# Softmax attention with a convolution beside it: conversion buffers in three spans, a longer late ring, 480 conversions

## The chip, the cores and the metric

The kernel runs on one core of one Trainium2 chip, in one launch. The core has five engines that run their own instruction queues and meet only at semaphores: TensorE (PE) for matmuls, VectorE (DVE), ScalarE (ACT), GpSimd (POOL) and SyncE (SP), which here only starts transfers. Matmuls write to PSUM; DVE and ACT read it, POOL does not use it in this kernel. The metric is the device time of one execution in microseconds (us), the median of several.

## The reference

```python
g = sigmoid((x * gate_w).sum(-1))                       # one gate a row
qkv = x @ wqkv                                          # x: 2048 x 512, 32 heads of 16
a = softmax(q @ k.T * 16 ** -0.5) @ v  ->  a @ wo       # each head 2048 x 2048
K = einsum("dn,dnl,dn->dl", C, exp(dt * A * l), dt * B).real   # 512 channels, 2048 long, 128 modes
b = causal_convolution(x, K) + x * Dskip
out = g * a + (1 - g) * b
```

The heavy part is the softmax: 32 x 2048 x 2048 exponentials. The second branch builds a convolution kernel K for each of the 512 channels out of powers of complex numbers, and applies it.

## The kernel before

**Attention.** Scores are computed in tiles of 128 keys x 512 queries of one head. A quad is four tiles: four heads on the same keys, one in each strip of 32 rows of PE. There are 512 quads (`NQ`), so 2048 tiles, in 32 blocks of 16 quads (a block is four heads and one quarter of the queries). The tiles stand in a list, three to a group; there are 683 groups (`NG`). `qk` computes the three score tiles of a group into one of two PSUM buffers (SC0 for even groups, SC1 for odd ones). `ex` (line 1037) turns them into bf16 exponentials with one ACT instruction, into slots of a ring. The ring is ET with `NS` slots of 512 columns, and from group `NSG` on also EX, which extends it to `NS2` slots. `seat` hands out the slots; a group's slots must lie together and may not straddle the border of ET and EX. `pv` multiplies the four tiles of a quad with the values (VE) and adds to the accumulator OA. The main loop at the end of `record` makes sure, before `ex` of a group, that the quads whose slots it overwrites have been through `pv`.

**Conversions.** Some tiles do not go to ACT. In a group that takes part, only two tiles are given to ACT, and the third is converted on DVE: `bits` (line 1059) computes scale x score + offset from PSUM into 16-bit integers, whose bits read as bf16 are already a rough exponential. Four converted tiles, the four heads of one quad, fill one buffer DZ; that is a set, and it takes part in four consecutive groups. `batch` (line 1078) makes three copies DU of the whole set with constants added to the integers, on POOL (in the last few groups on DVE, line 1074), and `sums` multiplies all four, DZ and the three DU, with the values, so that the errors of the four average out. Each set thus costs four conversions, three POOL adds and four quads of matmuls, and saves ACT four tiles.

**When a set may start.** `decide` builds the list of tiles as the main loop goes. `win` says in which span of groups (`WIN`: from, to, number of DZ buffers, number of DU buffers) a group lies, whether four groups have passed since the last set, whether the number of sets is below the pace (`PACE`, interpolated over groups), and whether the buffer is free (`room`). `DVCAP` bounds how much idle time of DVE may be used up, `STRX`, `STRE` and `STRK` say where a set may start near the end of a block.

**The convolution.** It is background work, laid between the groups: `params`, `bases`, `tables` and `kstage` build K in four quarters of four blocks of 32 channels (DVE products, among them the T products of line 1132, then matmuls into the PSUM buffer MB, then writes to DRAM); `xrows`, `yloads` and `ystage` load rows of x and of K (buffers U and H) and do the convolution in 32 units of 128 matmuls (`MB<-U,H`). At the end `outs` multiplies with `wo` and adds both branches. DMA starts of all of this go through SP's queue.

**What sets the order.** The kernel is a planner. Every piece of background work is a Python generator that announces an engine and a cost. `Sched.fill` simulates the five engines with fixed durations and, after each group's exponential, issues whatever fits until the time of the next; `Sched.force` issues work early when something is needed. Priorities are the numbers given at the start of each thread. So the order of every engine's queue is fixed when the kernel is built, and constants such as `TP`, `KP`, `OUTP`, `YLP`, `XGO`, `BG1` or `KEEP` only move work within it. PE also gets matmuls on a zero tile (`zero`, tile `wm`), so many that a target (`FILL`, after group `ZEND` `LOW`) of PE activity per group is met; `REST` forces a target on some groups up to a given one.

Of the kernel before, what the change touches and what calls it, by code (L numbers as in the profile page):

```python
# [15 lines left out]
S = 2048  # L16
# [40 lines left out]
NS = 20  # L57
NS2 = 24
NSG = 395
# [14 lines left out]
BG1 = 'g20'  # L74
BG2 = 'K3'
BG3 = 'K3'
TP = 0.86
KP = 0.85
NB = 2
NT = 2  # L80
TB = 4
# [3 lines left out]
US = [2, 12, 3]  # L85
HS = [4, 44, 8]
BACK = 0.66
# [12 lines left out]
KEEP = 8  # L100
FORE = 12
# [3 lines left out]
DVCAP = 8.7  # L105
# [5 lines left out]
STRX = 460  # L111
STRE = 640
# [642 lines left out]
def record(nc, p, B, ins):  # L755
# [7 lines left out]
    NSL = 4 * NQ  # L763
# [132 lines left out]
    plan = dict(q=0, at=0, used=0.0, prev=None, wait={}, x=0)  # L896
# [12 lines left out]
    def win(x):  # L909
        return next((w for w, (lo, hi, *_) in enumerate(WIN) if lo <= x < hi and x >= plan["x"] + 4 and len(sets) < due(x) and room(w)), None)  # L910

    def decide(g):
        while len(tiles) < min(3 * g + 3, NSL):
# [3 lines left out]
            if q + 2 < NQ and (kt < DVK - 1 or STRX <= x < STRE and kt in STRK) and win(x) is not None and idle() >= plan["used"] \  # L917
                    and (kt < DVL or not sets or f"dvp{len(sets) - 1}" in sch.flag):
                w = win(x)
                plan["x"] = x  # L920
                c = next(y for y in range(q, q + 3) if 0 < y % 16 < 15)
                a, b = [y for y in range(q, q + 3) if y != c]
# [3 lines left out]
                for _ in range(12):  # L926
                    if len(tiles) % 3 == 2:
                        vec[len(tiles) // 3] = (len(sets), k)
                        k += 1
                        tiles.append(late.pop(0))  # L930
                    else:
                        tiles.append(own.pop(0))
                plan["wait"][c // 16] = f"dvp{len(sets)}"
                n = sum(st["w"] == w for st in sets)
                r, nu = f"{w}{n % WIN[w][2]}", WIN[w][3]
# [15 lines left out]
            while todo and 4 * todo[0][0] + 3 in home:  # L951
                sch.add(pvq(*todo.pop(0)), 0, True)
# [1097 lines left out]
```

## Time and profile before

| | |
|---|---|
| median of 3 executions | 744.12 us (743.63, 744.12, 1048.6) |
| the profiled execution | 744.34 us |
| its span, first to last instruction | 742.5 us |
| granted TensorE clock, mean | 0.996 of full speed |
| conversions (line 1059) | 464, mean 684 ns |
| POOL adds (line 1078) | 345, mean 1045 ns |
| DMA | 94.89 MB, 128 GB/s over the span |

One of the three executions took 1048.6 us; the other two agree within 0.1%, and the median is one of them. The rows of the profile read as follows: a group of instructions has its line, engine, operation, `out<-in` by the names of the program, the tile shapes and the count; then the busy time of the group in us and the mean length of one instruction in ns; then the idle time of the engine just before them and what ended it. "PEld" is the loading of weights. Where instructions of one engine overlap, the busy time of a group is less than its count times the mean. A row of stretches gives from:to in us, the length, and busy times (with counts) of the engines that appear, then the granted clock, the share of DMA time and GB/s. A row of waits gives who waited for whom, us in total, times, and the longest.

### The profile page before, as it was taken

Reading aid. Unit: us, or ns where it says so; the run is one execution under the profiler, and the core shown is the slowest. Engines: PE = TensorE matmul, PEld = TensorE weight load, DVE = VectorE, ACT = ScalarE, POOL = GpSimd, SP = SyncE. Lnnn points to the kernel's source line nnn. Section 1 sums busy time; section 2 is a strip of 40 time slices with the busy share of each in tenths; the row PEclk is TensorE's granted clock in tenths of the full one; section 3 lists DMA queues with packets and bytes.
Section 4 is the critical chain, followed back from the end, with each engine's and each line's share of the span. In section 5 each row is a group of like instructions: output and inputs, shape, how many; then the busy total and the mean of one; then the engine's idle time right before and its main releaser. Section 6 shows DMA issues by size and latency. Waiting matters only on the chain.

```text
span 742.5 us, 31758 instructions
## 1 busy us (share of the span) xinstructions
PE 688.9 (93%) x14153; PEld 297.9 (40%) x14154; DVE 659.5 (89%) x1109; ACT 728.8 (98%) x696; POOL 363.1 (49%) x365
## 2 busy tenths in 40 slices
PE   8888788888899989999999999999999999999997
PEld 4333333333444444445444544544444442222222
DVE  6999999999999999899998988877888888898886
ACT  7999999999999999999999999999999999999996
POOL 4000000000026436555557556677888888888783
PEclk9999999999999999999999999999999999999999
DMA  9647931224656673343788586458877661001001
GB/s 217 154 108 164 177 40 41 62 52 130 167 128 183 175 214 84 91 126 80 214 226 228 156 221 170 130 112 198 218 159 183 164 153 49 19 19 27 19 15 38
DMA packets 148702, 94.89 MB, mean 128 GB/s; under 512 B 88338, under 2 KB 130004, under 8 KB 148564
## 3 DMA queue, kind: packets, MB, share of 16 engines
q1 hardware_dynamic: 147604, 91.99, 50.2%
q8 instruction: 111, 1.82, 1.1%
q10 hardware_dynamic: 960, 0.85, 0.4%
q14 instruction: 27, 0.22, 0.1%
HBM read 63.94 MB, written 18.90 MB: 112 GB/s over the span
## 4 chain that ended last, share of the span: by engine, by line
ACT 89%; PE 9%; DVE 1%; POOL 1%; issue 0%; DVEq 0%
ACT ET L1037 84%; ACT EX L1037 5%; PE SC L770 4%; PE OA L770 3%; PE MB L770 2%; POOL DU L1078 1%; DVE DZ L1059 0%; DVE Qm L1908 0%; DVE VE L880 0%; DVE Ks L1510 0%; DVE fo L2009 0%; DVE B L1341 0%; DVEq L732 0%; DVE wm L824 0%; DVE KT L1911 0%
## 5 line engine op out<-in xcount | busy, mean ns | idle before, releaser
L1037 ACT ACTIVATE ET<-SC 128x1024 bf16<-128x1024 f32 (+1 forms) x637 | 685.0, 1321 | 2.2 <-PE SC L770 1.9
L1078 POOL INT64_ADD DU<-DZ x345 | 355.6, 1045 | 364.5 <-DVE DZ L1059 263.8
L1059 DVE TENSOR_SCALAR DZ<-SC 128x512 uint16<-128x512 f32 x464 | 310.5, 684 | 60.0 <-PE SC L770 55.9
L770 PE MATMUL SC<-Qm,KT 32*128 32x512 bf16 x2048 | 271.6, 385 | 11.0 <-ACT ET L1037 7.5
L770 PE MATMUL OA<-ET,VE 128*32 128x512 bf16 x1490 | 153.5, 388 | 30.1 <-ACT ET L1037 29.4
L770 PEld LDWEIGHTS SC<-Qm,KT 32*128 32x128 bf16 x2048 | 68.9, 91 | 194.4 <-ACT ET L1037 124.6
L770 PE MATMUL OA<-DU,VE 128*32 128x512 bf16 x1392 | 134.5, 387 | 1.1 <-POOL DU L1078 1.1
L770 PEld LDWEIGHTS MB<-U,H 128*32 128x32 bf16 x4096 | 91.1, 143 | 29.3 <-issue 13.4
L770 PE MATMUL MB<-U,H 128*32 128x128 bf16 (+7 forms) x4096 | 96.5, 223 | 0.0
L770 PEld LDWEIGHTS OA<-ET,VE 128*32 128x32 bf16 x1490 | 39.6, 95 | 95.5 <-ACT ET L1037 52.0
L770 PE MATMUL OA<-wm 128*32 128x256 bf16 (+3 forms) x527 | 74.5, 344 | 1.2 <-DVE idf L825 1.2
L1132 DVE TENSOR_TENSOR T<-B,DT 128x1536 bf16<-128x1536 bf16 x64 | 62.3, 1013 | 0.0
L770 PEld LDWEIGHTS OA<-DU,VE 128*32 128x32 bf16 x1392 | 35.4, 95 | 50.9 <-issue 43.3
L1037 ACT ACTIVATE EX<-SC 128x1024 bf16<-128x1024 f32 (+1 forms) x46 | 50.5, 1227 | 0.0
L770 PEld LDWEIGHTS MB<-T,Z 128*32 128x32 bf16 x2048 | 42.1, 156 | 11.7 <-issue 9.0
L770 PE MATMUL MB<-T,Z 128*32 128x64 bf16 (+1 forms) x2048 | 45.9, 236 | 0.3 <-issue 0.3
L770 PE MATMUL OA<-DZ,VE 128*32 128x512 bf16 x464 | 45.8, 384 | 0.0
L1132 DVE TENSOR_TENSOR ft<-Z 128x512 f32<-128x512 f32 (+3 forms) x48 | 38.7, 829 | 0.3
L1132 DVE TENSOR_TENSOR Z<-ft,ft 128x1024 bf16<-128x1024 bf16 (+3 forms) x56 | 33.3, 595 | 0.5
L1099 DVE STREAM_TRANSPOSE OT<-OA 128x512 f32<-128x512 f32 x32 | 22.7, 709 | 1.8 <-PE OA L770 1.8
L770 PEld LDWEIGHTS OA<-wm 128*32 128x32 bf16 (+2 forms) x527 | 20.4, 96 | 9.4 <-issue 6.4
L1613 DVE TENSOR_TENSOR Yst<-MB,gt 128x512 bf16<-128x512 f32 x32 | 21.8, 680 | 1.8 <-PE MB L770 1.7
(141 smaller groups left out, 407.6 us busy)
## 6 DMA issues: line engine op xcount, KB each, us to landing
H<-gm_kd SPq DMA_DIRECT2D x128, 256.0 KB, 3.9
U<-gm_xs SPq DMA_DIRECT2D x128, 134.2 KB, 3.9
T<-B SPq DMA_DIRECT2D x16, 256.0 KB, 3.1
gm_yd<-Yst SPq DMA_DIRECT2D x16, 256.0 KB, 4.2
gm_kd<-Ks SPq DMA_DIRECT2D x64, 40.0 KB, 2.4
gm_xs<-xP SPq DMA_DIRECT2D x16, 136.0 KB, 7.0
gm_pd<-L SPq DMA_DIRECT2D x8, 256.0 KB, 3.6
Z<-gm_pd SPq DMA_DIRECT2D x8, 256.0 KB, 3.7
```

The costliest lines, as they stand in the source:

```text
L770: op("PE", lambda t: t.matmul(out(), lhsT(), rhs(), start=start, stop=stop, skip_group_check=True, **kw), R, W, c=c, lat=.15, a=a, cfg=cfg)
L1037: op("ACT", lambda a: a.activation(E(at, [[1, 512 * n]]), sc(0, [[1, 512 * n]]), AF.Exp, scale=DH ** -0.5), [(sc, i, g) for i in range(n)] ...
L1059: op("DVE", lambda v: v.tensor_scalar(z.u16(512 * k, [[1, 512]]), sc(1024, [[1, 512]]), XS, XB, ALU.mult, ALU.add), [(sc, 2, g)], [(z, k, ...
L1078: op("POOL", lambda v, u=u, cut=cut: v.int64_add(u.u64(), z.u64(), cut * 0x0001000100010001), R, [(u, 0, i)], c=1.016, lat=.09, lk=True)
L1099: op("DVE", lambda v: v.transpose(OT(512 * w, [[1, 512]]), OA(0, [[1, 512]])), [(OA, 0, b)], [(OT, w, b)], c=.64)
L1132: op(eng, lambda v: v.tensor_tensor(o(), a(), b_(), f), R, W, c=c)
L1613: op("DVE", lambda v, w=w, h=h: v.tensor_tensor(Yst(1024 * w + 4 * h, [[128, R8], [8, 16], [1, 4]]), MB(0, [[1, R8], [R8, 16], [NC, 4]]), ...
```

## The change

464 conversions become 480. They and all other work are planned anew with new constants, and the planner is extended:

- The buffers of the sets come in three spans of groups: up to 240 two DZ and four DU, from 240 three and five, from 460 four and six (before: two and four up to 480, then four and six). The pace, the bound on DVE's idle time and the groups where a set may start near the end of a block are new.
- The ring has 17 slots up to group 260 and 24 from there (before: 20 up to 395, then 24).
- The order of the four heads of a set is searched among all permutations (`order`) instead of taken from the table `JS`; tiles of the set's quads that are left when the fourth conversion is placed are kept (`rest`) and used in the next set.
- Conversions are numbered, and a new group's scores are preceded by the forced conversion of the PSUM buffer that they overwrite (`taken`) rather than by that of the group before the last. A second way to compute a third tile in a thread of its own (`qx`) exists for groups that are `apart` and for `EXTRA` sets; with the constants given, `EXTRA` is cut to an empty list and `apart` asks for a time later than 1e12 us.
- Background work: other start conditions and priorities; `TB` 8 instead of 4 (blocks below `TB` use one T buffer of their quarter, the others alternate between two); `KSEG` 2 instead of 4 (matmul steps planned together); the third U buffer from unit 10 instead of 12.
- Filler: `LOW` 1150 instead of 1200, `SURP` 128 instead of 192, `REST` no longer picks any group.

```diff
-PDEL = 0.43
+PDEL = 0.33
-OUTP = 3.78
+OUTP = 4.6
-KSEG = 4
+KSEG = 2
-LOW = 1200
-SURP = 192
+LOW = 1150
+SURP = 128
-OVER = (0.27, 0.64)
-REST = (13, 1, 1792, 425)
-DLAG = .6
+OVER = (0.34, 0.65)
+REST = (14, 0, 1792, 400)
+DLAG = 0.4
...
-NS = 20
+NS = 17
 NS2 = 24
-NSG = 395
+NSG = 260
...
-WIN = ((0, 480, 2, 4), (480, 679, 4, 6))
-PACE = ((0, 0), (61, 0), (78, 0.0), (149, 0.0), (206, 12.77), (270, 23.66), (340, 38.94), (414, 52.88), (500, 77.45), (564, 96.69), (630, 111.83), (683, 119.39))
-DVEND = 679
-YLP = 2
+WIN = ((0, 240, 2, 4), (240, 460, 3, 5), (460, 679, 4, 6))
+PACE = ((0, 0), (43, 0), (78, 0), (155, 0), (206, 10.72), (273, 23.49), (331, 40.86), (365, 49.17), (414, 61.07), (509, 79.68), (561, 101.98), (642, 118.74), (683, 126.74))
+DVEND = 4
+XR = (82, 84, 1, 8)
+APART = -1e12
+YLP = 3.83
-XGO = 'g19'
+XGO = 'g34'
-BG1 = 'g20'
-BG2 = 'K3'
-BG3 = 'K3'
-TP = 0.86
-KP = 0.85
+BG1 = 'g40'
+BG2 = 'K2'
+BG3 = 'K5'
+TP = 0.61
+KP = 0.03
-TB = 4
+TB = 8
-US = [2, 12, 3]
+US = [2, 10, 3]
-BACK = 0.66
+BACK = 0.34
-KEEP = 8
-FORE = 12
+KEEP = 4
+FORE = 16
-DVCAP = 8.7
+DVCAP = 6.75
-STRX = 460
-STRE = 640
+STRX = 440
+STRE = 680
...
-    NSL = 4 * NQ
+    EXTRA = [n for n in range(*XR[:2]) if (n - XR[0]) * XR[2] % XR[3] < XR[2]]
+    EXTRA = EXTRA[:len(EXTRA) // 6 * 6]
+    NSL = 4 * NQ - len(EXTRA)
...
+    def bank(x):
+        n, at = plan["conv"], plan["bank"]
+        old = taken.get(at)
+        taken[at] = n
+        plan["conv"], plan["bank"] = n + 1, 1 - at
+        return n, at, old
+
+    def order(own, more, c):
+        at = len(tiles)
+        best = None
+        for js in itertools.permutations(range(4)):
+            t, o, n = [x % 4 for x in tiles[at - at % 3:]], list(own), 0
+            k = bad = 0
+            while k < 4:
+                if len(t) % 3 == 2:
+                    t.append(js[k])
+                    k += 1
+                    bad += 3 - len(set(t[-3:]))
...
+                else:
+                    t.append(o.pop(0) % 4)
+            if best is None or bad < best[0]:
+                best = bad, js
+        return best[1]
...
-                own, late = [4 * a + k for k in range(4)] + [4 * b + k for k in range(4)], [4 * c + k for k in JS[len(tiles) % 3]]
-                js = JS[len(tiles) % 3]
+                own = plan["rest"] + [4 * y + k for y in qs for k in range(4)]
+                js = order(own, more, c)
+                late = [4 * c + k for k in js]
...
+            elif plan["rest"]:
+                qs = []
+                tiles.append(plan["rest"].pop(0))
...
-            if g - 1 in vec:
-                sch.force(f"bits{g - 1}")
+            at = vec[g + 1][3] if g + 1 in vec else (g + 1) % 2
+            old = vec[g + 1][4] if g + 1 in vec else taken.get(at)
+            if old:
+                sch.force(f"bits{old - 1}")
+            apart = g + 1 in vec and old is not None and done.get(old, 1e9) > p.tm["ACT"] - APART
+            if old is not None and not apart and (g + 1 in vec or len(slots(g + 1)) == 3):
+                sch.force(f"bits{old}")
```

More of the change, by code (lines that the diff above doesn't have):

```diff
@@ L1 @@
 from contextlib import ExitStack
+import itertools
 import math
@@ L895, in record @@
     todo = []
-    plan = dict(q=0, at=0, used=0.0, prev=None, wait={}, x=0)
+    plan = dict(q=0, at=0, used=0.0, prev=None, wait={}, x=-4, n=4, rest=[], conv=0, bank=0)
+    extra, taken, done = {}, {}, {}
     def idle():
@@ L909, in win @@
     def win(x):
-        return next((w for w, (lo, hi, *_) in enumerate(WIN) if lo <= x < hi and x >= plan["x"] + 4 and len(sets) < due(x) and room(w)), None)
+        return next((w for w, (lo, hi, *_) in enumerate(WIN) if lo <= x < hi and x >= plan["x"] + plan["n"] and len(sets) < due(x) and room(w)), None)
+    def bank(x):
[15 more added lines that the diff above has]
+                    bad += 3 - len(set(t[-3:]))
+                    if more and k == 2:
+                        bad += .1 * (js[k] in t[-3:])
+                        k += 1
+                else:
[3 more added lines that the diff above has]
+        return best[1]
     def decide(g):
@@ L916, in decide @@
             plan["used"] = max(plan["used"], idle() - DVCAP)
-            if q + 2 < NQ and (kt < DVK - 1 or STRX <= x < STRE and kt in STRK) and win(x) is not None and idle() >= plan["used"] \
+            more = len(sets) in EXTRA
+            n = -(-(8 - 2 * more - len(plan["rest"])) // 4) + 1
+            qs = range(q, q + n)
+            if not any(0 < y % 16 < 15 for y in qs):
+                n, qs = n + 1, range(q, q + n + 1)
+            if q + n - 1 < NQ and (kt < DVK - 1 or STRX <= x < STRE and kt in STRK) and win(x) is not None and idle() >= plan["used"] \
@@ L918, in decide @@
                     and (kt < DVL or not sets or f"dvp{len(sets) - 1}" in sch.flag):
                 w = win(x)
[L920 to L924 removed]
+                plan["x"], plan["n"] = x, 4 - more
@@ L925, in decide @@
+                c = next(y for y in qs if 0 < y % 16 < 15)
+                qs = [y for y in qs if y != c]
+                own = plan["rest"] + [4 * y + k for y in qs for k in range(4)]
+                js = order(own, more, c)
+                late = [4 * c + k for k in js]
                 k = 0
-                for _ in range(12):
+                while k < 4:
                     if len(tiles) % 3 == 2:
-                        vec[len(tiles) // 3] = (len(sets), k)
+                        vec[len(tiles) // 3] = (len(sets), k, *bank(len(tiles) // 3))
+                        tiles.append(late[k])
@@ L929, in decide @@
                         k += 1
-                        tiles.append(late.pop(0))
+                        if more and k == 2:
+                            extra[len(tiles) // 3 - 1] = (len(sets), k, *bank(len(tiles) // 3 - 1), late[k])
+                            k += 1
                     else:
                         tiles.append(own.pop(0))
+                plan["rest"] = own
                 plan["wait"][c // 16] = f"dvp{len(sets)}"
-                n = sum(st["w"] == w for st in sets)
@@ L952, in decide @@
                 sch.add(pvq(*todo.pop(0)), 0, True)
+        if g not in vec and len(slots(g)) == 3:
+            plan["bank"] = (g + 1) % 2
     def seat():
@@ L1930, in need @@
             sch.force(f"qm{b}")
-    ring = {}
+    ring, late = {}, {}
     lack = t0 = bare = 0
@@ L1941, in record @@
         sch.mark(f"g{g}")
+        for n, b in list(late.items()):
+            if b < at_slot(3 * g)[2]:
+                sch.force(f"bits{n}")
+            if f"bits{n}" in sch.flag:
+                del late[n]
         sch.mark(f"blk{at_slot(3 * g)[2]}")
@@ L1960, in record @@
             lack += p.act
-            qk(g + 1)
+            qk(g + 1, 2 if apart else None)
             if g + 1 in vec:
@@ L1965, in record @@
                     sch.force(f"dvp{i}")
-                sch.add(bits(g + 1), 0)
+                if apart:
+                    late[vec[g + 1][2]] = tiles[3 * g + 5] // 64
+                    sch.add(qx(g + 1, *vec[g + 1], tiles[3 * g + 5]), -1)
+                else:
+                    sch.add(bits(*vec[g + 1][:4], g + 1), -1)
+                if g + 1 in extra:
+                    late[extra[g + 1][2]] = extra[g + 1][5] // 64
+                    sch.add(qx(g + 1, *extra[g + 1]), -1)
         t = p.tm["ACT"]
```

42 lines of the change are left out of this document (26 added, 16 removed).

## The prediction

> **What bounds the kernel now.** I read the chain of waits first, then the exponentials grouped by shape, then the stretches of the span, and last the engines that the change loads.
>
> The page, with the busy times and the chain by engine:
>
> ```profile
> span 742.5 us, 31758 instructions
> ...
> PE 688.9 (93%) x14153; PEld 297.9 (40%) x14154; DVE 659.5 (89%) x1109; ACT 728.8 (98%) x696; POOL 363.1 (49%) x365
> ...
> ACT 89%; PE 9%; DVE 1%; POOL 1%; issue 0%; DVEq 0%
> ```
>
> ACT's groups by shape (count, then busy us, mean ns, idle us before them):
>
> ```profile
> L1037 ACT ACTIVATE ET<-SC 128x1024 bf16<-128x1024 f32 x421 | 398.8, 1169 | 0.7 <-PE SC L770 0.4
> L1037 ACT ACTIVATE ET<-SC 128x1536 bf16<-128x1536 f32 x216 | 295.6, 1617 | 1.5 <-PE SC L770 1.5
> L1037 ACT ACTIVATE EX<-SC 128x1024 bf16<-128x1024 f32 x44 | 47.1, 1205 | 0.0
> L1037 ACT ACTIVATE EX<-SC 128x1536 bf16<-128x1536 f32 x2 | 3.4, 1702 | 0.0
> ```
>
> The chain in order of time (start us, us, what), and from the timeline the last exponential:
>
> ```profile
> 11.06 1.46 ACT ET L1037
> ...
> 17.59 130.41 ACT ET L1037 x97
> ...
> 677.84 1.83 ACT EX L1037 x2
> 679.67 9.17 ACT ET L1037 x10
> ```
>
> ```profile
> 732.36 1.46 ACT L1037 ACTIVATE ET<-SC 128x1024 bf16<-128x1024 f32 x1
> ```
>
> The chain is 89% ScalarE (ACT): one exponential after another. All four shapes together sat idle only 0.7 + 1.5 = 2.2 us. Their length (1169, 1617 ns) isn't their cost, since neighbours overlap; the cost is the pitch in the chain. A group of three tiles takes 130.41 / 97 = 1.344 us, a group whose third tile is converted on VectorE (DVE) 9.17 / 10 = 0.917 us, and 1.83 / 2 = 0.915 us in the second buffer EX, so EX costs nothing extra. Check: 465 groups of two (421 + 44) x 0.917 + 218 of three x 1.344 = 719.4 us, against 722.8 us from the first exponential at 11.06 to the end of the last at 732.36 + 1.46 = 733.8 us; 2.2 us of the rest are the waits, and 1.2 two small activations in between. A converted tile is thus worth 1.344 - 0.917 = 0.427 us of the path, wherever it stands, as long as the others keep up.
>
> Where there are tiles left to convert is in the stretches:
>
> ```profile
> 11.06:148.10 137.04, 115.21 (x2504) 47.63 (x2504) 131.00 (x232) 136.50 (x104) 0.00 (x0) 0.99 0.56 112
> 148.10:305.00 156.90, 141.37 (x3323) 67.03 (x3324) 146.60 (x252) 156.90 (x138) 46.85 (x45) 1.00 0.53 140
> 213.00:483.00 270.00, 257.35 (x5995) 126.01 (x5995) 244.02 (x391) 268.99 (x264) 153.36 (x147) 1.00 0.61 165
> 305.00:483.00 178.00, 171.33 (x4003) 84.86 (x4007) 160.50 (x260) 176.99 (x175) 106.51 (x102) 1.00 0.62 166
> 483.00:711.00 228.00, 224.79 (x3932) 84.86 (x3924) 192.42 (x304) 228.00 (x249) 186.94 (x183) 1.00 0.44 108
> ```
>
> ```profile
> L1037 ACT ACTIVATE ET<-SC 128x1024 bf16<-128x1024 f32 x198 | 187.0, 1120 | 0.7 <-PE SC L770 0.4
> L1037 ACT ACTIVATE ET<-SC 128x1536 bf16<-128x1536 f32 x63 | 88.8, 1540 | 0.3 <-PE SC L770 0.3
> ...
> L1059 DVE TENSOR_SCALAR DZ<-SC x464: 624/690/694, 213.3 to 730.1; 128x512 uint16<-128x512 f32 x155
> ```
>
> Columns: stretch, length, then busy us of PE, PEld, DVE, ACT, POOL, granted clock, DMA share, GB/s. The two exponential rows are of 213 to 483 us. Conversions begin at 213.3 us. From there to 483 some 200 groups are converted and 64 are not (63 and one in EX); after 483 nearly all are. So the sixteen new conversions must come out of those 64, the stretch in which DVE is busy 244.02 of 270 us (90.4%) and idle 26.0.
>
> **The change part by part.**
>
> *Sixteen more conversions (464 to 480, four sets of four).* ACT: sixteen groups fall from 1.344 to 0.917 us, -16 x 0.427 = -6.8 us on the path.
>
> ```profile
> 717.91 1.90 DVE L1059 TENSOR_SCALAR DZ<-SC 128x512 uint16<-128x512 f32 x3
> L1059 DVE TENSOR_SCALAR DZ<-SC 128x512 uint16<-128x512 f32 x464 | 310.5, 684 | 60.0 <-PE SC L770 55.9
> L1078 POOL INT64_ADD DU<-DZ x345 | 355.6, 1045 | 364.5 <-DVE DZ L1059 263.8
> 545.51 0.40 PE L770 MATMUL OA<-ET,VE 128*32 128x512 bf16 x4
> 545.74 0.39 PE L770 MATMUL OA<-DU,VE 128*32 128x512 bf16 x4
> ```
>
> DVE: 16 x 0.684 = 10.9 us of busy time; queued back to back they take (1.90 - 0.684) / 2 = 0.608 us each, 9.7 us. The 26.0 us idle of the middle stretch cover it: 26.0 - 10.9 - 6.8 (the stretch gets shorter) = 8.3 us are left, 254.9 busy of 263.2 us, 96.8%. POOL: 12 adds x 1.045 = 12.5 us beside 153 of 270 busy, covered. PE: each set multiplies its four tiles four times (DZ and three DU) instead of once, three more quads of matmuls at 0.23 us (545.51 to 545.74), 12 x 0.23 = 2.8 us; cover is the filler below.
>
> ```profile
> 213.00:483.00 270.00, 30.51 (x226) 8.33 (x225) 0.00 (x0) 1.00 0.61 165
> 483.00:711.00 228.00, 0.28 (x4) 0.11 (x4) 0.00 (x0) 1.00 0.44 108
> L770 PE MATMUL MB<-U,H 128*32 128x128 bf16 (+7 forms) x4096 | 96.5, 223 | 0.0
> L1132 DVE TENSOR_TENSOR T<-B,DT 128x1536 bf16<-128x1536 bf16 x12 | 10.9, 944 | 0.0
> L1132 DVE TENSOR_TENSOR T<-B,DT 128x1536 bf16<-128x1536 bf16 x33 | 30.7, 978 | 0.0
> L1132 DVE TENSOR_TENSOR T<-B,DT 128x1536 bf16<-128x1536 bf16 x20 | 21.6, 1108 | 0.0
> ACT ET L1037 <- PE SC L770: 1.9, 5, 0.7
> ```
>
> *Filler.* The first two rows are PE's matmuls on the zero tile alone: 30.5 us in the middle stretch, 0.28 after. The change orders less of it (the forced groups go, the later target drops from 1200 to 1150). Without filler the granted clock was 1.00 from 483 to 711 us, so I cost less filler at nothing; it only frees PE.
>
> *Buffers of the sets* (three spans instead of two; from group 240 three DZ and five DU instead of two and four). No instruction is added. A set may start earlier, and the widened rule for the end of a block (groups 440 to 680) lets it too; nothing else waits for them. Cost nothing, gain counted above.
>
> *Ring of exponentials.* 17 slots instead of 20 up to group 260: five groups of three instead of six, 5 x 1.344 = 6.7 us from an exponential to the reuse of its slot, was 8.1. From 260 on 24 slots, split at 17, hold 8 + 3 = 11 groups of two; before it was ten up to group 395 and then twelve. ACT would wait for PE's matmuls on ET. No wait of that kind stands in the trace: ACT's exponentials waited for scores alone, 1.9 us in five places. Bounds: -1.9 (those go) and, by the same row, +1.9 (as many again). I take 0.
>
> *Head order.* At each of the three places in a group where a set can begin, trying all orders gives the list that was in the table: no two equal heads meet in a group before or after. Where leftover tiles run into the next set the new search keeps heads apart too. Nothing; the extra thread for a split third tile is never made, since its list comes out empty and its condition is never true.
>
> *Conversion queue.* A conversion is now forced by its score bank rather than by its group; banks alternate with the groups as before, so the same instruction waits for the same one. Nothing.
>
> *Background work moved.* Counts stay (64 T products, 128 loads each of U and H, 32 y units). The x rows start at group 34 instead of 19, 15 x 1.344 = 20 us later on SP's queue and on POOL (four memsets, in a stretch with POOL idle); the second quarter's base tables wait for group 40 instead of 20, the fourth's for K5 instead of K3; blocks 4 to 7 have one T buffer each in place of two, so DVE's T products of a block queue behind the K matmuls of the block ahead; U gets its third buffer at unit 10 instead of 12, which only lets a load go sooner. K steps are placed in pieces half as long. Who waits: y units on PE, then the output products. A y unit is 96.5 / 32 = 3.0 us of PE. Between 213 and 483 us filler covers ten of them; after 483 PE has 228 - 224.79 = 3.2 us idle, room for one. Bounds: 0 if at most one more unit slips past 483; three slipping cost 9.0 - 3.2 = +5.8. Less y work late is possible too, but PE then holds nobody, so no gain below 0. I take 0, since the first row has room for ten.
>
> *Contention.* The three T rows are of 11 to 148, 148 to 305 and 305 to 483 us: 944, 978, 1108 ns, with POOL busy 0, 46.85 and 106.51 us in them. I take 0 extra; the upper bound is the 33 of the middle row at the last row's price, 33 x 0.130 = 4.3 us of DVE. The Trainium skill says why it could come (GPSIMD Engine Reference, Key points): POOL shares its SBUF interfaces with VectorE and contends with DVE instructions that have two SBUF inputs, as these have. By that rule denser adds lengthen the T products; the trace agrees in direction, 944 to 1108 ns.
>
> *Start and end.* 11.1 us before the first exponential and 742.5 - 733.8 = 8.7 us after the last have the same instructions; 0.
>
> **Sum.** The profiled run took 744.34 us, its span 742.5; the rest around it, 1.8 us, stays. It lies 0.2 us above the median, 744.12, so I work from it. 744.34 - 6.8 = 737.5. Three engines now run above 90%, so I add 0.5 us for waits, about a quarter of the 1.9 us that stand now: 738.0 us, -0.8%. With all 2.2 us of waits gone it would be 735.3; with 1.9 us more, 739.4.
>
> **The rivals.**
>
> *PE takes part of it back (743 us).* Three y units past 483 us: 737.5 + 5.8 = 743.3. For it: no filler there, PE at 98.6%, later x rows, one T buffer. Against it: 30.5 us of filler before 483. ACT would then wait for scores late.
>
> *DVE nearly full (741 us).* The highest share that DVE reached is 131.00 / 137.04 = 95.6%. At that share the middle stretch needs 254.9 / 0.956 = 266.6 instead of 263.2 us: +3.4, 740.9. For it: 96.8% wanted. Against it: back-to-back conversions cost 0.608 and not 0.684 us, and base tables can move out of the stretch.
>
> *The same with contention (745 us).* The 4.3 us above on top: 259.2 / 0.956 = 271.1, +7.9, 745.4. The page named there is its ground. For it the 1108 ns row; against it that T work can be over sooner.
>
> *DVE stays at its present share: slower (756 us).* If conversions cannot be packed closer than now because each waits for its scores (55.9 of DVE's 60.0 us idle before them), DVE stays at 90.4%: 254.9 / 0.904 = 282.0, +18.8, 756.3. It is slower than before if DVE cannot pass 254.9 / 270 = 94.4%. Against it: 95.6% was reached, and waits for scores mean that DVE is early, not late.
>
> *It does not do what it says (744 us).* The converted groups move and ACT waits as long as it saved. Against it: in the stretch where all are converted ACT is busy 228.00 of 228.
>
> **How the numbers follow.** Forecast (735.3 to 739.5) 0.64; PE 0.14; DVE nearly full 0.10; with contention 0.03; DVE at its share 0.06, of which 0.03 over 759; no effect 0.03. The time is the forecast's, 738.0. The range 735.2 to 743.5 takes in the waits' bound below and the first two rivals and leaves out about one in eight. A difference of 2%, about what a measurement of this kernel can tell from no change, is 14.9 us (729.2 to 759.0): faster by more would need over twice the ACT time removed, 0.01; slower 0.03; within 0.96.
>
> **What would show it.** 481 exponentials of two tiles and 202 of three; 480 conversions, pitch still 0.917 and 1.344 us; ACT idle before exponentials under 4 us; DVE near 96% in the middle with fewer waits for scores; span near 736. I am wrong if ACT waits for scores or slots by more than 4 us, if y units pile up after 483 us with ACT waiting there, if T products exceed 1108 ns, or if the granted clock leaves 1.00.

## The result, and the profile after

| | before | after |
|---|---|---|
| median | 744.04 us (743.63 to 1048.6, 6 runs) | 740.08 us (738.44 to 740.78, 6 runs) |
| ratio to before | | 0.9939, 95% interval 0.9924 to 0.9954 |
| profiled execution, its span | 744.34, 742.5 us | 738.44, 736.6 us |
| first exponential starts, last one ends | 11.06, 733.8 us | 9.97, 727.5 us |

The change saves 0.6% of the time by the ratio, 4.0 us by the medians. One execution of before, 1048.6 us, was a slow one and is not in the ratio; without it before's median is 743.95 us. The profiled execution of after is the shortest of its six, so its own 5.9 us of span less are not all the change's.

The page of after, busy times and the chain that ended last by engine:

```profile
span 736.6 us, 31590 instructions
...
PE 681.0 (92%) x14058; PEld 299.2 (41%) x14058; DVE 665.2 (90%) x1125; ACT 722.6 (98%) x696; POOL 374.6 (51%) x377
...
ACT 84%; PE 14%; DVE 2%; issue 0%; POOL 0%; DVEq 0%; POOLq 0%
```

ACT's groups of after by shape (count, busy us, mean ns, idle us before them and what ended it):

```profile
L1095 ACT ACTIVATE ET<-SC 128x1024 bf16<-128x1024 f32 x372 | 353.4, 1140 | 1.9 <-PE OA L775 1.2 <-PE SC L775 0.6
L1095 ACT ACTIVATE ET<-SC 128x1536 bf16<-128x1536 f32 x196 | 266.7, 1671 | 0.5 <-PE SC L775 0.4
L1095 ACT ACTIVATE EX<-SC 128x1024 bf16<-128x1024 f32 x109 | 108.9, 1146 | 0.6 <-PE OA L775 0.2 <-PE SC L775 0.2
L1095 ACT ACTIVATE EX<-SC 128x1536 bf16<-128x1536 f32 x6 | 8.9, 1531 | 0.0
```

Its chain in order of time (start us, us, what), at the beginning, in the late part and at the end:

```profile
9.97 2.79 ACT ET L1095 x2
...
13.28 132.99 ACT ET L1095 x99
...
491.15 7.32 ACT ET L1095 x8
...
723.66 3.86 ACT ET L1095 x4
727.52 0.04 issue
```

Groups of two tiles are now 372 + 109 = 481, groups of three 196 + 6 = 202, and the pitches are as before, 7.32 / 8 = 0.915 us for a group of two and 132.99 / 99 = 1.343 us for a group of three. By the prediction's two pitches they come to 481 x 0.917 + 202 x 1.344 = 712.6 us, 6.8 less than before's 719.4. From the start of the first exponential to the end of the last pass 727.52 - 9.97 = 717.55 us, so 5.0 us lie between them that the pitches do not hold; before it was 722.8 - 719.4 = 3.4. The idle time in the rows rose from 2.2 to 1.9 + 0.5 + 0.6 = 3.0 us. Both figures hold the wait of the very first exponential, 0.66 us in before and 0.45 in after, which lies ahead of these 722.8 and 717.55 us; between the exponentials it is 1.5 and 2.6 us. The rest of the difference is that an exponential which had to wait does not overlap the one ahead of it. The share of ACT in the chain fell from 89 to 84%, PE's rose from 9 to 14.

So the 5.9 us of span split into three: the start 1.1 us sooner, the exponentials 722.8 - 717.55 = 5.2 us shorter, and what follows the last of them 9.1 instead of 8.7 us. The start was a matter of this execution and not of the change. Here are eight small matmuls near the start, of before and then of after, from the timeline (start us, us, what):

```profile
4.80 1.82 PE L770 MATMUL SC<-idb,x0n 128*128 128x128 bf16 x8
```

```profile
4.48 1.05 PE L775 MATMUL SC<-idb,x0n 128*128 128x128 bf16 x8
```

The same eight small matmuls took 1.82 us in one profile and 1.05 us in the other: the full clock is recorded from 6.43 us on in before and from 3.99 us on in after. In the kernel that the last experiment below shows they took 1.86 us, with its first exponential at 11.11 us. Before also had a stretch at clock 0.50 (second row), behind one in which PE was busy 2.02 of 3.42 us (first row); just after it a group waited 0.54 us for its scores:

```profile
9.84:13.26 3.42, 2.02 (x42) 0.92 (x44) 2.65 (x6) 2.76 (x3) 0.29 (x2) 1.00 1.09 282
13.26:16.67 3.41, 3.16 (x71) 1.65 (x63) 2.10 (x4) 3.41 (x4) 0.00 (x0) 0.50 1.15 137
```

Without the start (1.1 us, and the 0.6 us by which that group came late) the profiles differ by 4.2 us, close to the 4.0 of the medians: -6.8 from the exponentials, +2.2 from new waits between them, +0.4 at the end.

The stretches of after (from:to, length, then busy us of PE, PEld, DVE, ACT, POOL, clock, DMA share, GB/s), and in the last two rows the zero-tile matmuls alone:

```profile
213.00:483.00 270.00, 258.73 (x5979) 128.20 (x5976) 249.39 (x409) 267.81 (x270) 165.98 (x162) 1.00 0.63 168
483.00:711.00 228.00, 225.15 (x3997) 87.66 (x3989) 195.25 (x309) 227.62 (x247) 188.70 (x184) 1.00 0.44 105
```

```profile
213.00:483.00 270.00, 23.19 (x128) 6.13 (x128) 0.00 (x0) 1.00 0.63 168
483.00:711.00 228.00, 0.59 (x8) 0.21 (x8) 0.00 (x0) 1.00 0.44 105
```

DVE is busy 249.39 of 270 us, 92.4%, not more than it can do. ACT's waits of after, as the view of waits has them (who waited for whom, us, times, longest):

```profile
ACT fo L2087 <- PE MB L775: 4.0, 1, 4.0
...
ACT ET L1095 <- PE OA L775: 1.2, 2, 0.9
ACT ET L1095 <- PE SC L775: 1.0, 3, 0.4
ACT EX L1095 <- PE OA L775: 0.2, 1, 0.2
ACT EX L1095 <- PE SC L775: 0.2, 1, 0.2
```

The exponentials wait for PE alone, and the longest wait is at group 264, where the sums change from one block to the next. Three rows of the timeline around it:

```profile
329.75 0.71 DVE L1157 STREAM_TRANSPOSE OT<-OA 128x512 f32<-128x512 f32 x1
...
330.51 0.40 PE L775 MATMUL OA<-ET,VE 128*32 128x512 bf16 x4 [0.56 <-DVE OT L1157]
...
330.95 1.94 ACT L1095 ACTIVATE ET<-SC 128x1024 bf16<-128x1024 f32 x2 [0.95 <-PE OA L775]
```

At the end of a block DVE takes the sums out of OA (OT), and the first matmuls of the next block may not write OA before that. DVE had just been converting; the transpose came late, PE stood 0.56 us, and ACT, whose next slots that matmul still read, 0.95 us behind it. This is read from the trace; no run took the conversions or the transpose away.

### The profile page after: what moved, and what is told of

It is laid out like the page before. It is cut to its first block, busy times and chain, and to the rows that moved or that the text cites. A ratio compares the mean times of both kernels' runs of the same rounds, so it can differ in the third digit from the quotient of the medians.

```text
span 736.6 us, 31590 instructions
## 1 busy us (share of the span) xinstructions
PE 681.0 (92%) x14058; PEld 299.2 (41%) x14058; DVE 665.2 (90%) x1125; ACT 722.6 (98%) x696; POOL 374.6 (51%) x377
## 4 chain that ended last, share of the span: by engine, by line
ACT 84%; PE 14%; DVE 2%; issue 0%; POOL 0%; DVEq 0%; POOLq 0%
ACT ET L1095 72%; ACT EX L1095 11%; PE OA L775 6%; PE SC L775 5%; PE MB L775 3%; DVE DZ L1116 1%; POOL DU L1136 0%; DVE OT L1157 0%; DVE Yst L1671 0%; DVE OnT L1182 0%; DVE Qm L1966 0%; DVE fo L2084 0%; ACT ea L1253 0%; DVE B L1190 0%; DVE ON L1180 0%
## 5 line engine op out<-in xcount | busy, mean ns | idle before, releaser
L1095 ACT ACTIVATE ET<-SC 128x1024 bf16<-128x1024 f32 (+1 forms) x568 | 615.0, 1323 | 2.4 <-PE OA L775 1.2
L1136 POOL INT64_ADD DU<-DZ x357 | 367.1, 1044 | 348.3 <-DVE Ks L1571 214.1
L1116 DVE TENSOR_SCALAR DZ<-SC 128x512 uint16<-128x512 f32 x480 | 321.5, 685 | 52.8 <-PE SC L775 49.9
L775 PE MATMUL OA<-ET,VE 128*32 128x512 bf16 x1332 | 137.4, 387 | 36.3 <-ACT ET L1095 34.6
L775 PE MATMUL OA<-DU,VE 128*32 128x512 bf16 x1440 | 137.8, 386 | 1.0 <-POOL DU L1136 0.8
L1095 ACT ACTIVATE EX<-SC 128x1024 bf16<-128x1024 f32 (+1 forms) x115 | 116.9, 1166 | 0.6 <-PE OA L775 0.2
L775 PE MATMUL MB<-U,H 128*32 128x128 bf16 (+7 forms) x4096 | 98.7, 223 | 0.4 <-issue 0.4
L775 PEld LDWEIGHTS OA<-ET,VE 128*32 128x32 bf16 x1332 | 35.7, 94 | 95.7 <-ACT ET L1095 57.7
L775 PE MATMUL OA<-wm 128*32 128x512 bf16 (+3 forms) x423 | 67.6, 350 | 1.2 <-DVE idf L830 1.2
L775 PEld LDWEIGHTS MB<-T,Z 128*32 128x32 bf16 x2048 | 44.9, 155 | 13.7 <-issue 9.7
L775 PE MATMUL OA<-EX,VE 128*32 128x512 bf16 x236 | 31.2, 386 | 0.0
```

Source lines behind the costliest of these rows:

```text
L775: op("PE", lambda t: t.matmul(out(), lhsT(), rhs(), start=start, stop=stop, skip_group_check=True, **kw), R, W, c=c, lat=.15, a=a, cfg=cfg)
L1095: op("ACT", lambda a: a.activation(E(at, [[1, 512 * n]]), sc(0, [[1, 512 * n]]), AF.Exp, scale=DH ** -0.5), [(sc, i, g) for i in range(n)] ...
L1116: op("DVE", lambda v: v.tensor_scalar(z.u16(512 * k, [[1, 512]]), sc(1024, [[1, 512]]), XS, XB, ALU.mult, ALU.add), [(sc, 2, ("d", n))], [ ...
L1136: op("POOL", lambda v, u=u, cut=cut: v.int64_add(u.u64(), z.u64(), cut * 0x0001000100010001), R, [(u, 0, i)], c=1.016, lat=.09, lk=True)
```

## The experiments

Each is a change to the kernel after unless said. They ran on four chips, each beside before on the same chip, where before's median lay between 743.87 and 744.96 us; differences to the kernel after, 740.08 us, may be across chips. Of the questions left the first was whether the conversions earn their price, the second where the 2.2 us of new waits come from, and the third what else of the change matters.

**Late conversions taken away again.** The sets end at 116, so the last sixteen groups that were converted go to ACT whole; the rest stays as planned.

```diff
-... and len(sets) < due(x) and room(w)), None)
+... and len(sets) < min(due(x), 116) and room(w)), None)
```

> The changed kernel with at most 116 sets, so 464 conversions; its first 116 sets are as they were, and the last 16 groups that were converted go to ScalarE whole. If each converted tile is worth its 0.427 us of ScalarE wherever it stands (the forecast's step), the time rises by 16 x 0.427 = 6.8 us to about 747, above the kernel before. If the late, fully converted stretch is held by TensorE (no filler there, 98.6% busy) and not by ScalarE, less comes back: 3 us or less, about 743.

Measured: 747.45 us (747.05 to 749.5), ratio to before 1.0045 (1.0029 to 1.0061), 7.4 us over the kernel after. Sixteen groups at 0.427 us are 6.8. In its profile the exponentials take 726.2 us, first to last, 8.7 more than in after, so there is more in it than the price. Two rows of stretches at the end (same columns as above):

```profile
718.14:721.56 3.42, 1.88 (x26) 0.52 (x22) 0.00 (x0) 3.42 (x4) 0.00 (x0) 1.00 0.00 0
721.56:738.62 17.06, 16.15 (x153) 3.92 (x149) 0.00 (x0) 14.44 (x11) 0.00 (x0) 0.50 0.00 1
```

With the conversions gone PE had pauses there, the clock was halved, and nine groups of three from 720.71 to 734.14 us stand 1.49 us apart instead of 1.344, 1.3 us in all. Two waits that after's profile lacks, 0.53 and 0.60 us at groups 345 and 351, add 1.1 us, and one of 0.38 us at group 517 is gone. So the run agrees with the price of a conversion also at the end, but the 7.4 us are not the price alone; and with before's number of conversions nothing of the gain is left.

**The new constants with before's spans.** Only `WIN` is put back; 464 conversions come out.

```diff
-WIN = ((0, 240, 2, 4), (240, 460, 3, 5), (460, 679, 4, 6))
+WIN = ((0, 480, 2, 4), (480, 679, 4, 6))
```

> The changed kernel with the two spans of set buffers of before (two DZ and four DU up to group 480). Its plan falls back to 464 conversions, with all other constants new. If the spans carry the sixteen conversions and nothing else matters, the time rises by 16 x 0.427 = 6.8 us to about 747. If the new waits (2.3 us more idle of ScalarE than before) come from the density of conversions in the middle stretch, they go with them and the time is about 744.5. If the other constants alone are a gain, it is under 743.

Measured: 747.19 us (743.79 to 748.71), ratio 1.0028 (1.0005 to 1.0051). The three spans carry the sixteen conversions; without them the rest of the change gains nothing. That it loses a little need not be the constants as such: in its profile 2.3 us of waits stand in groups 349 to 352, around a stretch at half clock (415.89 to 422.71 us).

**Before's constants with three spans.** The reverse, an edit of the kernel before; 472 conversions.

```diff
-WIN = ((0, 480, 2, 4), (480, 679, 4, 6))
+WIN = ((0, 290, 2, 4), (290, 480, 3, 5), (480, 679, 4, 6))
```

> The kernel before with nothing changed but three spans of buffers (two and four up to group 290, three and five up to 480, then four and six): 472 conversions. If spans alone make the gain: eight conversions more at 0.427 us, 3.4 us less, median 740.8 us, ratio 0.995 to 0.996. If a set only pays when the rest of the work is laid anew with it (as where the other constants were put without the spans, or the spans with a later border): the exponentials' phase gets shorter but waits or work behind the last exponential take it back, median 744 us or more.

Measured: 750.15 us (746.72 to 752.06), ratio 1.0065 (1.0042 to 1.0089). Eight conversions more, and 5.5 us over the 744.66 us of before on the same chip: the rival. Two rows of stretches (same columns as above) and two waits of its trace, the first within 614 to 628 us, the second at the end:

```profile
619.47:622.89 3.42, 1.74 (x54) 1.13 (x57) 1.11 (x3) 1.77 (x3) 3.02 (x4) 1.00 0.77 237
622.89:626.30 3.41, 3.41 (x77) 1.54 (x74) 2.42 (x5) 2.54 (x4) 0.07 (x1) 0.50 0.60 177
```

```profile
PE MB L770 <- DMA H<-gm_kd: 1.8, 1, 1.8
...
ACT fo L2012 <- PE MB L770: 7.2, 1, 7.2
```

PE's queue holds a convolution unit whose operand H is late; the scores behind it wait too, and after a window in which PE was busy 1.74 of 3.42 us the clock is halved for the next. The wait of the last cast, 7.2 us, was 3.7 in before. First to last the exponentials take 726.7 us, 4.0 more than in before, where eight conversions should take 3.4 off; the place shown has some 2.5 us of it, other new waits of up to 1.0 us are spread over six more groups. With before's other constants the spans alone gain nothing.

**More conversions still.** `FORE` 12 instead of 16 and the middle span up to 500: 488 conversions.

```diff
-WIN = ((0, 240, 2, 4), (240, 460, 3, 5), (460, 679, 4, 6))
-FORE = 16
+WIN = ((0, 240, 2, 4), (240, 500, 3, 5), (500, 679, 4, 6))
+FORE = 12
```

> The changed kernel with eight more conversions, 488 (one constant of TensorE's background placement back to 12, the middle span of buffers up to group 500). If each is worth 0.427 us the time falls by 3.4 us to about 736.7. Rival theory: past some density the conversions are given back as waits, since each set brings TensorE three more quads of matmuls and DVE four conversions ahead of block changes; then ScalarE's idle time before exponentials grows from 3.0 to 6 us or more and the time is 740 to 743.

Measured: 742.92 us (740.58 to 745.36), ratio 0.9978 (0.996 to 0.9996), 2.8 us over the kernel after. The exponentials, first to last, take 714.4 us, 3.1 less than in after, nearly the eight conversions' 3.4. The rival expected waits between the exponentials; what took the gain back was the end:

```profile
ACT fo L2087 <- PE MB L775: 10.3, 1, 10.3
```

**The forced filler put back.** `REST = (13, 1, 1792, 425)` as in before; the new plan has 484 conversions.

```diff
-REST = (14, 0, 1792, 400)
+REST = (13, 1, 1792, 425)
```

> The changed kernel with one of its rules put back: every thirteenth group up to 425 gets forced filler (target 1792) and no convolution work on TensorE. The plan then holds 484 conversions, four more. By the forecast's step (filler costs nothing, a conversion is worth 0.427 us) the time falls by 1.7 us to about 738.4. Rival: TensorE has no time to give in the dense middle stretch; work pushed out of those groups makes scores late elsewhere, ScalarE's idle time grows by more than 5 us and the time is 744 or more in spite of four more conversions.

Measured: 746.57 us (745.49 to 749.26), ratio 1.0038 (1.0023 to 1.0053). Again the exponentials are shorter than in after, 715.4 us, and the end is longer, 18.1 instead of 9.1 us; the rival has the time right, but not the waits that it expected. The timeline of DVE behind the last exponential of this kernel, with the last cast's wait:

```profile
726.54 0.69 DVE L1800 TENSOR_TENSOR fo<-MB,Yl 128x512 bf16<-128x512 f32 x1 [0.61 <-PE MB L775]
728.67 0.69 DVE L1800 TENSOR_TENSOR fo<-MB,Yl 128x512 bf16<-128x512 f32 x1 [1.44 <-PE MB L775]
...
733.11 0.69 DVE L1800 TENSOR_TENSOR fo<-MB,Yl 128x512 bf16<-128x512 f32 x1 [1.52 <-PE MB L775]
```

```profile
ACT fo L2087 <- PE MB L775: 13.1, 1, 13.1
```

Four output products that in after are done beside the exponentials now stand behind them, 2.2 us apart, and the cast waits 13.1 us instead of 4.0. From 483 us on PE is 98.7% busy in after (225.15 of 228): work that slips into this part has no room but at the end.

**The longer ring from group 240.** The order of all instructions stays; only the slots change.

```diff
+        m = NS2 if g >= 240 else NS
+        if at + n > m:
+            at = 0
...
+        at = (at + n) % m
```

> The changed kernel with every engine's queue in the same order, but the ring of exponentials has its 24 slots from group 240 instead of 260 (17 before), so a slot is reused after eleven groups instead of eight. Theory: the 1.06 us that ScalarE lost at group 264 was a wait for TensorE's matmul that freed a slot of the short ring; it goes, and the time falls by about 1.0 us, with the other waits unchanged. Rival: TensorE is late there by itself (block change, sums waiting for POOL), and the next scores come as late: the wait moves by a few groups and the time stays within 0.3 us.

Measured: 741.48 us (738.92 to 742.49), ratio 0.9952 (0.9935 to 0.997), no difference from the kernel after. Rows of its timeline, PE and then ACT:

```profile
332.19 0.40 PE L780 MATMUL OA<-ET,VE 128*32 128x512 bf16 x4 [0.56 <-DVE OT L1162]
```

```profile
332.95 1.02 ACT L1100 ACTIVATE EX<-SC 128x1024 bf16<-128x1024 f32 x1 [0.35 <-PE SC L780]
334.36 1.02 ACT L1100 ACTIVATE EX<-SC 128x1024 bf16<-128x1024 f32 x1 [0.39 <-PE SC L780]
```

With more slots group 264 no longer waits for a slot, but PE still stands 0.56 us behind the transpose, and the next two groups wait for scores instead. The wait only moved by a group; the ring isn't its cause. The profile is 3.1 us longer than that of after for other reasons: its first exponential starts at 11.45 us, 1.5 later, and two waits of 0.66 and 0.59 us stand at groups 345 and 351. PE pauses there in the middle of a convolution unit, and the profile shows nothing that it waits for. The run above without the last sixteen conversions has the same two; after's profile, its shortest execution, has neither.

**Seven eighths of the convolution's matmuls left out, everywhere.** The output lacks most of the convolution.

```diff
+            if isinstance(tag, tuple) and tag[0] == "y":
+                k = seen[tag] = seen.get(tag, -1) + 1
+                if k % 32 >= 4:
+                    continue
```

> The changed kernel in the same order, but seven of eight matmuls of the 32 convolution units (MB from U and H) are left out, so the convolution part of the output is incomplete; about 84 of 96 us of TensorE go, DVE and POOL keep all their work. If TensorE's load makes ScalarE's new waits for scores (groups 311, 331, 384, 418, 517), they go and the sum of ScalarE's idle time before exponentials falls from 3.0 to under 1.5 us; span about 735. If DVE, with conversions ahead of block changes and evictions, makes them, they stay: span within 0.5 us of 736.6 at the same start.

Measured: 743.27 us (741.73 to 747.57), ratio 0.9996 (0.9977 to 1.0015). The time answers nothing: with so much less to do PE had pauses, the mean granted clock of the profile fell to 0.984, and new waits came where the clock was halved. Of the five waits named, four are gone in its trace or nearly so (0.11 us at group 418), and the fifth, at 331, lies in a stretch at half clock (394.89 to 401.72 us).

**The same, but only ahead of the waits.** Seven eighths of the convolution's matmuls are left out in the five groups ahead of groups 311, 318, 331, 375, 384, 418 and 517 alone, the seven other places where an exponential of after comes late.

```diff
+        near = {q for g in (311, 318, 331, 375, 384, 418, 517) for q in range(g - 5, g)}
...
+                if k % 32 >= 4 and q in near:
+                    continue
```

> The changed kernel in the same order, but in the five groups ahead of each of seven waits (groups 311, 318, 331, 375, 384, 418, 517) seven of eight convolution matmuls are left out, so part of the convolution is missing from the output; elsewhere all of them stay, so that TensorE's clock should hold. If convolution work planned close ahead of scores makes those waits, the seven (2.2 us together in the changed kernel's trace) shrink to under 0.5 us and the wait at group 264 stays at 1.06. If DVE makes them, they stay.

Measured: 737.66 us (736.74 to 738.57, two executions), ratio 0.9909 (0.9878 to 0.9941). ACT's waits in its trace:

```profile
ACT ET L1103 <- PE OA L783: 0.9, 1, 0.9
ACT ET L1103 <- PE SC L783: 0.4, 1, 0.4
```

Six of the seven waits are gone, the one at 418 is smaller (0.11 us), and the one at 264 (first row), which was left alone, stands as it was; the second row is the wait of the very first exponential. The exponentials take 715.7 us, first to last, 1.85 less than in after. So the convolution's matmuls close ahead of the scores make these waits: over the middle PE has room, 23.19 us of filler, but not in each group.

**Without filler.** All zero-tile matmuls after the first group are left out.

```diff
-        log = prog.log
+        log = [(f, q, a) for f, q, a in prog.log if not (a[0] == "PE" and q >= 0 and a[2] and a[2][0][0].name == "wm")]
```

> The changed kernel in the same order without any matmul on the zero tile after the first group (the zeros add nothing, so the result is the same). The forecast's step: filler costs nothing and holds nothing, so the time stays, or falls by up to 1 us where filler stood ahead of scores, and the granted clock stays 1.00. Rival, by the rule of the Trainium skill that an idle window halves the clock (TensorE: Matmul & The Clock Gate, Part 1): in the early stretch, where filler is 28 of 115 us of TensorE's busy time, the clock drops in places, TensorE gets late there and the time rises by 3 us or more.

Measured: 743.5 us (741.48 to 748.69), ratio 0.9993 (0.9974 to 1.0011), 3.4 us over the kernel after. Two stretches of its trace, columns as above:

```profile
119.68:123.09 3.41, 2.13 (x29) 0.65 (x29) 3.21 (x6) 3.41 (x4) 0.00 (x0) 1.00 0.35 115
123.09:126.50 3.41, 3.41 (x30) 0.63 (x22) 3.41 (x6) 3.05 (x3) 0.00 (x0) 0.50 0.00 0
```

PE was busy 2.13 of 3.41 us in a stretch, and in the next the clock was 0.50; this came seven times between 123 and 267 us, twice for 6.83 us. From 266 us on, to the last exponential, the clock stayed 1.00 without filler; up to 483 us PE was busy 208.38 of 216.55 us there. So filler isn't free to drop everywhere: it is needed where PE's own work leaves pauses.

**An improved kernel, first attempts.** With some twenty planning constants chosen anew (`LOW`, `SURP`, `FILL`, `PACE`, `DVCAP`, `LAZY`, `FAIR`, `TP`, `YLP`, `BACK`, `OUTP`, `STRE` among them) 488 and 484 conversions fit with the end of after. The spans of the two:

```diff
-WIN = ((0, 240, 2, 4), (240, 460, 3, 5), (460, 679, 4, 6))
+WIN = ((0, 241, 2, 4), (241, 510, 3, 5), (510, 679, 4, 6))
```

> 488 conversions once more, but with the background work laid so that the output products fit beside the late exponentials (other values of some twenty planning constants, computation unchanged). First theory (a conversion pays its 0.43 us in the phase of the exponentials, and what e8 gave back was only work pushed behind the last exponential): first to last exponential 714 to 715 us, the cast's last wait for MB back at 4 to 5 us, median 736 to 738 us, ratio to before 0.989 to 0.992. Rival (eight more conversions always push work of PE or DVE past the end, wherever the rest is laid): the last wait 8 us or more and the median 740 to 743 us. A second rival (less filler and other places bring waits between exponentials): last wait 4 us, but the phase 717 us or more, median 739 to 741 us.

```diff
-WIN = ((0, 240, 2, 4), (240, 460, 3, 5), (460, 679, 4, 6))
+WIN = ((0, 240, 2, 4), (240, 469, 3, 5), (469, 679, 4, 6))
```

> 484 conversions, other values of some twenty planning constants, computation unchanged. First theory: half of the gain of the 488 above, first to last exponential about 716 us, the last wait for MB about 4 us, median 738 to 739 us, ratio 0.991 to 0.993. Rivals as above: last wait 8 us or more, or more waits between exponentials, median 740 us or more.

Measured: 488 conversions 741.12 us (740.23 to 744.15), ratio 0.9963 (0.9947 to 0.9979); 484 conversions 746.28 us (743.69 to 747.74), ratio 1.0018 (1.0001 to 1.0034). The ends were short, as wanted: the last cast waited 3.3 and 4.5 us. But PE starved, in the 488 at one place, in the 484 at several. The 488's timeline, PE, ACT and SP's queue:

```profile
614.63 0.66 PE L778 MATMUL MB<-U,H 128*32 128x128 bf16 x32 [2.83 <-DMA H<-gm_kd]
```

```profile
615.87 1.02 ACT L1098 ACTIVATE EX<-SC 128x1024 bf16<-128x1024 f32 x1 [3.00 <-PE SC L778]
```

```profile
596.61 5.67 SPq L1770 DMA_TRANSPOSE OnR<-gm_od  x4
602.32 1.09 SPq L1774 DMA_DIRECT2D Wo<-in_A_wo_dram  x2
603.46 2.38 SPq L1777 DMA_DIRECT2D Wr<-in_A_wo_dram  x4
605.95 0.56 SPq L1630 DMA_DIRECT2D U<-gm_xs  x1
606.62 1.01 SPq L1642 DMA_DIRECT2D H<-gm_kd  x1
```

Four transposed loads hold SP's queue 5.67 us, six loads of wo and one of x 4 us more, and only then come the loads of H. The queue's order is not all of it: the load of H that starts at 606.62 us took 7.8 us to land, where the loads of H take 4.0 at the median; at that it would have been there by 610.6 us, before PE came to it at 611.8. Why it landed so late the trace doesn't show. PE waits 2.83 us with the scores queued behind, and the clock is halved from 615.27 to 618.69 us; the phase of the exponentials is 720.1 us instead of the 714 to 715 wanted, some 4 of it at these three groups. In the 484's a group of PE's matmuls waited 3.4 us for DVE (VE) at 58 us, and DVE itself had stood 4.7 us behind a DMA (gm_pd<-M); group 36 waited 4.0 us for its scores, and two windows at half clock followed.

**The late load put right.** The first of the two, with the loads of H from unit 50 on planned as landing 6 us after their start. Seven other planning constants (`OUTP`, `SURP`, `PACE`, `YLP`, `KEEP`, `DVCAP`, `FAIR`) and the placing of the buffers in memory were chosen anew with it, so it is a new plan and not a test of the load alone.

```diff
-..., c=.66, lat=3.5, b=HB / HN, pace=True)
+..., c=.66, lat=(6 if u >= 50 else 3.5), b=HB / HN, pace=True)
```

> The 488 conversions of e10_488 with one step undone that its trace shows: at group 561 TensorE stood 2.8 us for a load of H (256 KB, started late because four transposed loads, six loads of wo and a load of x stood ahead of it in SP's queue), the clock fell to 0.5 for 3.4 us behind it, and the exponentials of groups 561 to 563 waited 4.15 us. Here the loads of H from unit 50 on are counted as landing 6 us after their start instead of 3.5, with a few planning constants chosen again for it; computation unchanged. First theory (that wait alone stood between e10_488 and its gain): no wait over 1 us near group 561, clock 1.0 there, first to last exponential 715.5 to 717 us, the cast's last wait 3 to 5 us, span 733.5 to 735.5 us, median 736 to 738 us, ratio 0.989 to 0.991. Rival (SP's queue and the DMA engines are the bound late in the kernel: another load comes late instead): a wait of 1 us or more behind a DMA at another group, or a last wait of 6 us or more, median 739 us or more.

Measured: 736.87 us (736.29 to 738.35), ratio 0.9896 (0.9873 to 0.9919), which beats before by 1.0% and the kernel after as well (the intervals, 0.9873 to 0.9919 and 0.9924 to 0.9954, do not meet; each against before on its own chip). Two waits, the clock where it had fallen, and SP's queue:

```profile
ACT fo L2090 <- remote: 3.9, 1, 3.9
...
ACT EX L1098 <- PE SC L778: 1.4, 2, 1.1
```

```profile
615.27:618.69 3.42, 3.42 (x80) 1.59 (x76) 2.78 (x5) 3.42 (x5) 3.19 (x4) 1.00 0.81 256
```

```profile
605.27 2.71 SPq L1630 DMA_DIRECT2D U<-gm_xs  x3
608.09 2.15 SPq L1642 DMA_DIRECT2D H<-gm_kd  x3
```

The order of SP's queue is much the same, and the load of H that starts at 608.09 us still takes 7.3 us to land, but the convolution now makes a pause in PE's queue there: its matmuls stop at 611.1 us and go on at 615.9 us, with scores and sums between them. No exponential waits there, and all of them take 716.5 us, first to last. The longest wait between them, 1.1 us (second row), is at group 365, 427.6 us: PE stood 1.09 us within a convolution unit, again with nothing in the profile that it waited for, so a load as its cause, which the rival names, is not shown. The span, 736.5 us, is above the 733.5 to 735.5 expected: the profiled execution had the late clock shown above (first exponential at 11.11 us) and was the longest of the four.

## Why the prediction was right

The forecast, 738.0 us, was 2.1 us below the median, 740.08, which lies within the stated range (735.2 to 743.5) but above the 739.5 that closes the forecast's own row. As a number 740.08 is nearer to the row "DVE nearly full (741)", whose mechanism did not come. That the profiled span is 736.6 us, as foreseen, is luck: it is the shortest of six executions. Of the terms of the time one was mis-sized.

*Sixteen conversions, -6.8 us:* right. The counts and pitches are those foreseen, and the kernel without them is 7.4 us slower, about 1.3 of it by the half clock at its end.

*The 0.5 us for waits:* this is the step that was too small. It was taken as a quarter of before's waits on ACT, a number that shows no mechanism, and 0.66 of those 1.9 us lie ahead of the first exponential. The runs showed +2.2 us between the exponentials and +0.4 at the end: 0.95 us is the wait at group 264, by the trace PE behind DVE's transpose at a block change, and most of the rest PE's own load in short stretches, shown by leaving matmuls out ahead of the waits. That is the rival "PE takes part of it back" in kind, but in the middle and not by units slipping past 483 us: ACT is busy 227.62 of 228 us there.

*Ring, 0:* right in size. Waits for slots, of which before had none, do stand in after (`<- PE OA`, 1.2 + 0.2 = 1.4 us, within the bound of 1.9); at the longest of them more slots only move the wait by one group.

*Filler, 0:* right for the amount that was cut, 30.5 to 23.2 us in the middle. It isn't a rule: without any the kernel loses 3.4 us. The reason given, a granted clock of 1.00 without filler after 483 us, held without filler from 266 us on; between 123 and 267 us the clock fell seven times. The Trainium skill ("TensorE: Matmul & The Clock Gate", Part 1) has the clock fall after an idle window of about 3.4 us. The length agrees, 3.41 us; but PE was not idle in these windows, it was busy 2.13 and 1.74 of some 3.4 us, so here pauses within a window were enough.

*Buffers, head order, queue of conversions, 0 by themselves:* nothing in the runs speaks against it, but none was tested alone. With before's spans the new constants gave 1.0028 of before's time.

*Background moved, 0:* right for this plan, and by little. Other plans let the end work slip, and the cast's last wait was 10.3 and 13.1 us instead of 4.0, a loss of 6 and 9 us.

*DVE nearly full:* did not come. From 213 to 483 us there are 222 conversions instead of 200, more than the sixteen counted, and yet DVE is at 92.4% and not 96.8%, among other things because fewer T products lie there, 28 instead of 32, and each is shorter (985 instead of 1078 ns).

*Contention, 0:* right. T products of after in the stretches 148 to 305 and 305 to 483 us:

```profile
L1190 DVE TENSOR_TENSOR T<-B,DT 128x1536 bf16<-128x1536 bf16 x36 | 33.1, 961 | 0.0
L1190 DVE TENSOR_TENSOR T<-B,DT 128x1536 bf16<-128x1536 bf16 x12 | 11.5, 988 | 0.0
```

They did not lengthen (978 and 1108 ns before), though POOL does more; only four late ones, after 483 us, stand at 1122 ns. That is over the 1108 that the prediction gave as a sign of being wrong, but DVE is busy only 195.25 of 228 us there. The bound of 4.3 us was far off.

*Start and end, 0:* the end grew by 0.4 us. The start differs by up to 1.5 us from one profile to the next.

## What to carry to other kernels

Where one engine's chain sets the time, work taken off it earns its price per piece; what is given back shows in other places, here in waits behind a neighbour that is full for a few groups at a time and behind the last link. Look for what is pushed past the end of the chain as much as for waits in it, and for a late operand: in a queue that keeps its order a single late load stops everything behind it. Filler that holds the clock may go only where the engine's own work leaves few pauses.

## What had not been expected of the hardware

The full clock is granted at a moment that differs from one execution to the next: eight small matmuls at the start took 1.05 us in one profile and 1.82 or 1.86 in others. In the fourteen profiles of these kernels it is recorded first between 3.99 and 7.22 us, and the first exponential starts between 9.97 and 11.45 us, later as a rule where the clock came later. The executions of after lie 2.3 us apart, and a good part of that may be this and half-clock stretches: the two with a mean granted clock of 0.999 and 1.000 took 738.44 and 738.75 us, the four with 0.996 or 0.997 took 739.65 to 740.78.

The clock is halved for 3.41 us or a multiple of it (17.06 us at the end of the kernel without the last sixteen conversions) behind a window in which PE made pauses, and how long PE was busy in that window does not decide it alone. Windows in which it was busy 0.64, 1.74, 1.88, 2.02 and 2.13 of some 3.4 us were followed by 0.50, and so was one of 2.82 of 3.42 us (412.48 to 415.90 us, in the kernel with before's spans); yet in the last kernel one of 2.84 of 3.41 us (611.86 to 615.27) kept 1.00, and so did 2.66 and 2.54 of some 3.4 us in after (7.40 to 10.80, 10.82 to 14.23). What is counted stays open.
